# Batch 0 of an attention, mixture and Fourier kernel: q and k loaded as whole rows over two queues and turned by TensorE

## The chip, the cores and the metric

The kernel runs on one core of a Trainium2 chip. The metric is the time of one execution in device microseconds. A profile shows one execution; its span runs from the first to the last instruction, and that execution's own time is a little longer than its span.

## The reference

Three stages follow each other, in float32 (the weights of the second and third stage come as 8-byte numbers and are narrowed on the chip):

```python
# q, k, v: batch 4, 8 heads, 576 positions, head size 64
q_d, k_d, v_d = (mean over 4 neighbouring positions of q, k, v)          # 144 positions
out_up    = repeat(softmax(q_d k_d^T / 8) v_d, 4)
out_local = softmax(q k^T / 8, masked to |i - j| < 4) v
x = out_up + out_local                     # (4, 576, 512)
h = relu(x @ w_in);  u, v = halves of h;  v_n = layernorm(v)
x = (u * (w_spatial @ v_n + b_spatial)) @ w_out
u = x + real(fft2(x))
out = u + relu(layernorm(u) @ w_ch1) @ w_ch2
```

Both score products of the attention need q and k with the head size on the partitions, that is, turned: in memory a position's 64 numbers lie side by side.

## The kernel before

The attention works in halves: batch b, group g of four heads. A half has four tiles of 128 partitions by 576 columns (two of q, two of k, two heads in each: partitions 0 to 63 and 64 to 127). The steps of a half are short functions, named in an order string (`ORD0` for batch 0): T turns a tile, PD pools it over four positions (POOL), BS makes the masked local scores and their softmax, PS the pooled ones, BA and PA turn the probabilities, BV and PV multiply by v and add into `xf`, the attention's output of the batch.

`moe(b)` is the second and third stage up to the Fourier transform of batch b. It is nearly all TensorE work: each product is done as three matmuls on a high and a low part (`mm3`, lines 138 to 141). The attention of batch b+1 is woven into moe(b) by a planner (`Filler`) that deals out steps by costs given in the code. The feed-forward (`ffn_gen`) comes last. Before moe(0) can start, the attention of batch 0 has to be done (both of its halves run interleaved, lines 1065 to 1077) and w_in has to be brought into `winh` and `winl`.

Loads are issued by SP, in program order: all eight q/k tiles of batch 0 first (line 1051), then v in two layouts (`vb`, `vp`) mixed with the sixteen loads of w_in into eight staging pieces (`prep_fetch`, lines 1052 to 1062), then q, k and v of batch 1. A q/k tile comes in by four DMAs (`qk_load`, line 326), each of which takes 32 of a head's 64 columns: runs of 32 numbers, 128 bytes, laid so that a transposition of 32x32 blocks within DVE (line 406) ends with the head size on the partitions.

w_in is narrowed piece by piece (`narrow`, lines 118 to 130: one ACT operation at 124, three DVE operations at 125, 126 and 128), then ACT casts the high part into `winh` (line 198) and POOL subtracts for the low part in `winl` (line 185).

The order in which an engine gets its instructions is set when the program is built, by a scheduler that follows a simulated timeline; on the chip each engine then works in that order. PSUM tiles of the first half come from the tags `tp` (two banks), `sc` (two) and `av` (one), those of the second half from `mm` (three).

Of the kernel before, what the change touches and what calls it, by code (L numbers as in the profile page):

```python
# [9 lines left out]
F32 = mybir.dt.float32  # L10
F32R = mybir.dt.float32r
# [8 lines left out]
P = 128  # L20
# [2 lines left out]
EPS = 1e-6  # L23
RATIO = [0.35, 0.5, 0.55, 0.5]
QK, T2 = 7, 6
EARLY = 12
PREP0 = 18
BVE = 'aa'
# [16 lines left out]
def tile_attn_moe_fft_mixer(  # L45
# [18 lines left out]
    nc = tc.nc  # L64
    B, H, S, D = q.shape
# [9 lines left out]
    big = ctx.enter_context(tc.tile_pool(name="big", bufs=1))  # L75
# [10 lines left out]
    def bank(tag, shape):  # L86
        n = 1
        for s in shape[1:]:
            n *= s
        t = ps.tile([P, 512], F32, tag=tag, name=tag, bufs={"mm": 3, "tp": 2, "sc": 2, "av": 1}[tag])  # L90
        t = t[:shape[0], :n]
        if len(shape) == 3:
            t = t.rearrange("p (a b) -> p a b", a=shape[1])
        elif len(shape) == 4:
            t = t.rearrange("p (a b c) -> p a b c", a=shape[1], b=shape[2])
        return t
# [18 lines left out]
    def wide(src):  # L115
        return 1 if src.dtype == F32 else 2

    def narrow(raw, n, scratch=None):
        w = raw.rearrange("p (n two) -> p n two", two=2)
        m = t2(n) if scratch is None else scratch[0]  # L120
        mi = m.bitcast(I32)
        a = t2(n) if scratch is None else scratch[1]
        ai = a.bitcast(I32)
        nc.scalar.mul(m, w[:, :, 1], 2.0 ** -112)  # L124
        nc.vector.tensor_scalar(ai, mi, 3, 0x7FFFFFF8, op0=ALU.logical_shift_left, op1=ALU.bitwise_and)  # L125
        nc.vector.scalar_tensor_tensor(ai, in0=mi, scalar=-2 ** 31, in1=ai, op0=ALU.bitwise_and,  # L126
                                       op1=ALU.bitwise_or)
        nc.vector.scalar_tensor_tensor(ai, in0=w[:, :, 0].bitcast(I32), scalar=29, in1=ai,  # L128
                                       op0=ALU.logical_shift_right, op1=ALU.bitwise_or)
        return a  # L130
# [13 lines left out]
    ident = ident_r.bitcast(F32)  # L144
# [7 lines left out]
    folds = const.tile([97, 66], F32R, name="folds")  # L152
    fold, fold_o = folds[:, 0:33], folds[:, 33:66]

    winh = big.tile([P, 4, 1024], F32R, tag="winh", name="winh")
    winl = big.tile([P, 4, 1024], F32R, tag="winl", name="winl")
    wsh_, wf_, ds_, dd_ = [], [], [], []

    u2_d = [[dram.tile([S, DM], F32, name=f"u2_d{b}_{i}") for i in range(4)] for b in range(B)]
# [24 lines left out]
    def prep_lo(lo, w, hi):  # L184
        LOENG.tensor_tensor(lo, w, hi.bitcast(F32), op=ALU.subtract)

    def prep():
        dbl = wide(w_in)
        sg = big.tile([P, 4, 512], F32, tag="wfl", name="scratch")
        prev = None  # L190
        for n in range(8):
            h, kk = 1 - n // 4, n % 4
            c = slice(h * 512, (h + 1) * 512)
            w = stage[n][:, :512 * dbl]
            if dbl == 2:
                w = narrow(w, 512, (sg[:, 2 * (n % 2), :], sg[:, 2 * (n % 2) + 1, :]))
            hi = winh[:, kk, c]
            nc.scalar.copy(hi, w)
            if prev is not None:
                prep_lo(*prev)  # L200
            prev = (winl[:, kk, c], w, hi)
            yield
        prep_lo(*prev)
        yield
# [78 lines left out]
    ready = {}  # L283
# [7 lines left out]
    def aux(kind, alt, m=None):  # L291
        shape, bufs = SPEC[kind]
        if not alt:
            t = ap_.tile(shape, F32, tag=kind, name=kind, bufs=bufs)
        else:
            tag, off, n = ALT[kind]
            if tag not in alt_tiles:
                alt_tiles[tag] = big.tile([P, ALTSZ[tag]], F32, tag=tag, name="alt_" + tag)
            size = 1
            for x in shape[1:]:  # L300
                size *= x
            i = alt_n.get(kind, 0)
            alt_n[kind] = i + 1
            o = off + (i % n) * size
            t = alt_tiles[tag][:shape[0], o:o + size]
            if len(shape) == 3:
                t = t.rearrange("p (a b) -> p a b", a=shape[1])
            elif len(shape) == 4:
                t = t.rearrange("p (a b c) -> p a b c", a=shape[1], b=shape[2])
        return t if m is None else t[:, 0:m]  # L310
# [3 lines left out]
    def is_alt(b, g):  # L314
        return b == 0 and g == 1

    extra = {}

    def qk_load(b, g, t):
        x = aux("qk", is_alt(b, g))  # L320
        src, hp = (q, k)[t % 2], t // 2
        for h2 in range(2):
            for dh in range(2):
                pt = 64 * h2 + 32 * dh
                h = b * H + 4 * g + 2 * hp + h2
                nc.sync.dma_start(x[pt:pt + 32].rearrange("p (j c) -> p j c", c=32),  # L326
                                  bass.AP(src.tensor, h * S * D + 32 * dh, [[D, 32], [32 * D, S // 32], [1, 32]]))
        ready["n", b, g, t] = x
# [30 lines left out]
    UNITS = [(0, 1), (2, 3), (4,)]  # L359
    bg = [(b, g) for b in range(B) for g in range(2)]  # L360
    loader = {"n": qk_load, "vp": vp_load, "vb": vb_load}
    queues = {}
    for alt in (False, True):
# [10 lines left out]
    def abank(tag, alt, shape):  # L374
        return bank("mm" if alt else tag, shape)
# [20 lines left out]
    def half(b):  # L396
        st = {}
# [4 lines left out]
            return xf_t[b]  # L402

        def t_(g, t):
            x = ready.pop(("n", b, g, t))
            nc.vector.transpose(x, x)  # L406
            st["qk", g, t] = x
# [112 lines left out]
        def bv_out(g, u, av, m):  # L520
# [13 lines left out]
            else:  # L534
                acc(xs[:, :, 467:525], av[:, :, 0, 3:61])
                acc(xs[:, :, 525:576], av[:, :, 1, 13:64])

        return {"T": (t_, .1), "PD": (pd, 0.2), "PS": (ps_, 1.0), "PA": (pa, .5), "PV": (pv, .95), "BS": (bs, 3.0),
                "BA": (ba, .45), "BV": (bv, 2.7)}

# [520 lines left out]
    for _ in pf:  # L1061
        pass
    pr = itertools.chain(prep(), prep_sp())
    atg = attention()
    ga, gb = head_half(0, bg[2]), head_half(1, None)
    live = [ga, gb]
    n = early = 0
    while live:
        for x in list(live):
            if next(x, "end") == "end":  # L1070
# [2 lines left out]
        if n > PREP0:  # L1073
            next(pr, None)
        if ga not in live and early < EARLY:
            next(atg)
            early += 1
    for _ in pr:
        pass
    for _ in range(EARLY - early):  # L1080
        next(atg)
# [91 lines left out]
```

## Time and profile before

| | |
|---|---|
| median of 3 runs | 865.77 us (861.98 to 866.14) |
| the profiled execution: its time, its span | 863.39 us, 861.6 us |
| busy in the span | PE 804.5, DVE 485.9, ACT 304.5, POOL 192.4 us |
| mean granted TensorE clock | 0.972 of full speed |
| moved by DMA | 71.84 MB in 154209 packets, 122805 of them under 512 B |
| first matmul of moe(0) | 79.31 us |

Times are microseconds from the span's start. PE is TensorE's matmuls, PEld its weight loads, DVE is VectorE, ACT ScalarE, POOL GpSimd, SP the engine that issues most of the DMAs. A slice of the page is a fortieth of the span, 21.5 us; its digit is the busy share in tenths.

### The profile page before, as it was taken

To read this page: it belongs to the slowest core of one execution; us is meant where nothing else is said; L and a number is where in the kernel's file an instruction comes from. 1 tells how busy PE (TensorE), PEld (TensorE's weight loads), DVE (VectorE), ACT (ScalarE), POOL (GpSimd) and SP (SyncE) were. 2 spreads that over 40 slices of the span, in tenths; PEclk is the share of its full clock that TensorE was granted. 3 is DMA by queue.
4 is the path that set the end of the run, shared out by engine and by line. 5 is a ranking of instruction groups with operands and counts; after the bars stand their busy time and mean duration, and the time that the engine had idled before them with its cause. 6 is when DMAs were issued, how large, how long until landed. Compare 5 with 4: busy or idle time off the path is not lost.

```text
span 861.6 us, 14351 instructions
## 1 busy us (share of the span) xinstructions
PE 804.5 (93%) x5309; PEld 664.9 (77%) x5309; DVE 485.9 (56%) x1109; ACT 304.5 (35%) x929; POOL 192.4 (22%) x237
## 2 busy tenths in 40 slices
PE   3658999999999999999799889999999999999998
PEld 1547888778977897899587667888888888888897
DVE  3798899587578846669749995223222322221211
ACT  1764774445363627334524552111110111111011
POOL 4457522224123310133504552000000000000000
PEclk9677999999999999999899899999999999999999
DMA  7788364433233110152406552322121222110100
GB/s 121 186 175 191 73 141 114 83 88 62 53 70 92 38 33 1 35 174 70 152 22 201 187 172 75 109 49 58 40 98 40 59 49 83 40 25 0 49 1 25
DMA packets 154209, 71.84 MB, mean 83 GB/s; under 512 B 122805, under 2 KB 140822, under 8 KB 154140
## 3 DMA queue, kind: packets, MB, share of 16 engines
q1 hardware_dynamic: 152668, 65.63, 31.0%
q0 software_dynamic: 1472, 5.30, 1.9%
q8 instruction: 42, 0.69, 0.3%
q14 instruction: 27, 0.22, 0.1%
HBM read 58.83 MB, written 12.07 MB: 82 GB/s over the span
## 4 chain that ended last, share of the span: by engine, by line
PE 75%; DVE 12%; SPq 4%; issue 3%; DMA 3%; ACT 2%; POOL 1%; DVEq 0%; ACTq 0%; POOLq 0%
PE mm L139 15%; PE mm L140 14%; PE mm L141 14%; PE tp L141 4%; PE tp L139 4%; PE tp L140 4%; PE sc L139 3%; PE sc L140 3%; PE sc L141 3%; SPq L326 2%; DVE t L128 2%; PE sc L433 2%; DVE t L126 2%; DVE t L125 1%; PE sc L481 1%
## 5 line engine op out<-in xcount | busy, mean ns | idle before, releaser
L964 DVE SCALAR_TENSOR_TENSOR hl<-mm,hh 128x512 fp32r<-128x512 f32 (+1 forms) x80 | 50.9, 636 | 220.2 <-ACT hh L589 220.2
L589 ACT ACTIVATE hh<-mm 128x512 fp32r<-128x512 f32 (+1 forms) x80 | 44.3, 554 | 264.6 <-PE mm L141 260.0
L599 POOL TENSOR_TENSOR rs<-ve,nhalf 128x1 f32<-128x1 f32 (+1 forms) x38 | 25.3, 679 | 251.0 <-DVE ve L598 246.8
L386 ACT ACTIVATE eb<-sc,mx 128x64 f32<-128x64 f32 x140 | 41.7, 340 | 32.2 <-DVE mx L384 32.1
L139 PE MATMUL mm<-xgh,winh 128*128 128x288 f32 x128 | 39.2, 307 | 0.0
L139 PE MATMUL mm<-wfh,xgh 128*128 128x512 f32 (+1 forms) x80 | 33.8, 423 | 5.4 <-ACT yx L705 5.3
L139 PE MATMUL mm<-wsh,vnh 128*128 128x288 f32 x128 | 38.4, 300 | 0.0
L140 PE MATMUL mm<-xgl,winh 128*128 128x288 f32 x128 | 38.2, 298 | 0.0
L141 PE MATMUL mm<-xgh,winl 128*128 128x288 f32 x128 | 38.1, 297 | 0.0
L140 PE MATMUL mm<-wsl,vnh 128*128 128x288 f32 x128 | 38.0, 297 | 0.0
L141 PE MATMUL mm<-wsh,vnl 128*128 128x288 f32 x128 | 38.0, 297 | 0.0
L128 DVE SCALAR_TENSOR_TENSOR t<-raw,t 128x512 int32<-128x512 int32 x32 | 36.3, 1134 | 0.0
L406 DVE STREAM_TRANSPOSE qk<-qk 128x576 f32<-128x576 f32 x28 | 21.7, 775 | 23.3 <-DMA qk<-in_q_dram 12.8
L386 ACT ACTIVATION_READ_ACCUMULATOR eb<-sc,mx 128x1 f32 x140 | 32.6, 233 | 0.0
L140 PE MATMUL mm<-wfl,xgh 128*128 128x512 f32 (+1 forms) x80 | 32.5, 409 | 0.0
L423 POOL TENSOR_TENSOR ta<-qk 128x288 f32<-128x288 f32 x28 | 22.9, 818 | 40.1 <-DVE qk L406 34.0
L141 PE MATMUL mm<-wfh,xgl 128*128 128x512 f32 (+1 forms) x80 | 31.3, 410 | 0.0
L816 POOL DMA_INDIRECT u_d<-t,idx x12 | 15.6, 1298 | 61.9 <-DVE t L809 55.6
L124 ACT ACTIVATE t<-raw 128x512 f32<-128x512 f32 x32 | 21.3, 671 | 20.7 <-DMA raw<-in_moe_w_ch_dram 11.6
L411 POOL TENSOR_TENSOR vp<-vp 72x512 f32<-72x512 f32 x13 | 17.8, 1368 | 45.8 <-DMA vp<-in_v_dram 45.8
L481 PE MATMUL sc<-qk 64*64 64x64 f32 x560 | 20.4, 246 | 8.0 <-DMA qk<-in_q_dram 3.9
L383 DVE TENSOR_REDUCE mx<-sc 72x2 f32<-72x288 f32 (+2 forms) x49 | 24.3, 506 | 5.1 <-PE sc L433 4.4
(526 smaller groups left out, 2525.9 us busy)
## 6 DMA issues: line engine op xcount, KB each, us to landing
raw<-in_moe_w_ch_dram SPq DMA_DIRECT2D x32, 512.0 KB
out_dram<-t SPq DMA_DIRECT2D x18, 256.0 KB
qk<-in_q_dram SPq DMA_DIRECT2D x56, 72.0 KB
qk<-in_k_dram SPq DMA_DIRECT2D x56, 72.0 KB
vp<-in_v_dram SPq DMA_DIRECT2D x26, 144.0 KB
vb<-in_v_dram SPq DMA_DIRECT2D x56, 64.0 KB
u2t<-u_d SPq DMA_DIRECT2D x10, 256.0 KB
t<-u_d SPq DMA_DIRECT2D x10, 256.0 KB
```

The costliest lines, as they stand in the source:

```text
L128: nc.vector.scalar_tensor_tensor(ai, in0=w[:, :, 0].bitcast(I32), scalar=29, in1=ai, op0=ALU.logical_shift_right, op1=ALU.bitwise_or)
L139: nc.tensor.matmul(out, lhsT=ah, rhs=bh, start=first, stop=False)
L140: nc.tensor.matmul(out, lhsT=ah, rhs=bl, start=False, stop=False)
L141: nc.tensor.matmul(out, lhsT=al, rhs=bh, start=False, stop=last)
L383: nc.vector.reduce_max(mx, sc, axis=AX.X)
L386: nc.scalar.activation(e[:, i, :], sc[:, i, :], AF.Exp, bias=mx[:, i:i + 1], scale=sc_in, accum_out=sm[:, i:i + 1])
L406: nc.vector.transpose(x, x)
L423: E['pd'].tensor_tensor(a, x[:, 0::2], x[:, 1::2], op=ALU.add)
L481: nc.tensor.matmul(scs[u][c, z, :], lhsT=x[2 * hp][o, s:s + 64], rhs=x[2 * hp + 1][o, s:s + 64], start=False, stop=(i == 2 * m - 1 and hp ...
L589: nc.scalar.activation(dst, src, AF.Relu)
L599: nc.gpsimd.tensor_tensor(rs, ve, nhalf[:rows], op=ALU.pow)
L964: last[0] = nc.vector.scalar_tensor_tensor(hl[:, :n], in0=ph, scalar=0.0, in1=hh[:, :n].bitcast(F32), op0=ALU.max, op1=ALU.subtract)
```

## The change

The q and k tiles of batch 0 (both halves) are loaded otherwise and turned otherwise; those of batches 1 to 3 stay. A tile is now loaded by two DMAs, one head each, the first issued by SP and the second by ACT. A partition takes nine neighbouring positions of a head, all 64 columns of each: one run of 576 numbers, 2304 bytes. These raw rows lie in the memory of `winl` (seven tiles) and `winh` (the eighth); `winh` and `winl` themselves are therefore allocated later, in `prep`. Step T of batch 0 (`qk_turn`) takes 18 matmuls against the identity (nine positions by two heads, 64x64 each) into two PSUM tiles, and two copies, of five positions by ACT and of four by DVE, that write to every ninth column. The main loop now draws the four T steps of both halves ahead of everything else, and the counter that starts the preparation of w_in starts at 4 to match.

```diff
-    winh = big.tile([P, 4, 1024], F32R, tag="winh", name="winh")
-    winl = big.tile([P, 4, 1024], F32R, tag="winl", name="winl")
+    winh = winl = None
...
     def prep():
+        nonlocal winh, winl
+        winh = big.tile([P, 4, 1024], F32R, tag="winh", name="winh")
+        winl = big.tile([P, 4, 1024], F32R, tag="winl", name="winl")
...
+    homes = {}
+
+    def qk_rows(b, g, t):
+        src, hp = (q, k)[t % 2], t // 2
+        n = 4 * g + t
+        tag = "winl" if n < 7 else "winh"
+        if tag not in homes:
+            homes[tag] = big.tile([P, 4096], F32, tag=tag, name="rows_" + tag)
+        raw = homes[tag][:, S * (n % 7):S * (n % 7) + S]
+        for h2 in range(2):
+            h = b * H + 4 * g + 2 * hp + h2
+            (nc.sync, nc.scalar)[h2].dma_start(raw[64 * h2:64 * h2 + 64],
+                                               bass.AP(src.tensor, h * S * D, [[S, 64], [1, S]]))
+        ready["n", b, g, t] = raw
+
+    def qk_turn(b, g, t):
+        raw = ready.pop(("n", b, g, t))
+        x = aux("qk", is_alt(b, g))
+        xr = x.rearrange("p (s r) -> p r s", r=NR)
+        for r0, n, copy in ((0, 5, nc.scalar.copy), (5, 4, nc.vector.tensor_copy)):
+            tp = abank("tp", is_alt(b, g), [P, n, 64])
+            for r in range(n):
+                for h2 in range(2):
+                    o = slice(64 * h2, 64 * h2 + 64)
+                    nc.tensor.matmul(tp[o, r, :], lhsT=raw[o, (r0 + r) * D:(r0 + r + 1) * D], rhs=ident[o, o],
+                                     start=True, stop=True)
+            copy(xr[:, r0:r0 + n, :], tp)
+        return x
+
     def qk_load(b, g, t):
+        if b == 0:
+            qk_rows(b, g, t)
+            return
...
         def t_(g, t):
+            if b == 0:
+                st["qk", g, t] = qk_turn(b, g, t)
+                return
...
-    n = early = 0
+    for x in live:
+        for _ in range(4):
+            next(x)
+    n, early = 4, 0
```

## Rows read from the trace of the kernel before

**Rows 1.** The page's slices: PE, tenths busy in each fortieth of the span.

```profile
PE   3658999999999999999799889999999999999998
```

**Rows 2.** Table by stage: busy us (instructions) per engine, clock, DMA share, GB/s.

```profile
0.00:28.00 28.00, 11.80 (x152) 8.27 (x152) 10.64 (x24) 7.50 (x37) 10.58 (x26) 1.00 0.77 138
...
35.00:80.00 45.00, 31.63 (x354) 24.44 (x353) 43.68 (x86) 30.74 (x107) 28.59 (x26) 0.69 0.84 178
80.00:861.60 781.60, 758.92 (x4772) 630.18 (x4770) 425.90 (x989) 262.63 (x766) 150.09 (x184) 0.99 0.29 75
```

**Rows 3.** Timeline of PE: start, duration, instructions, idle time before and its releaser.

```profile
9.16 0.69 PE L481 MATMUL sc<-qk 64*64 64x64 f32 x8 [3.87 <-DMA qk<-in_q_dram]
13.24 1.98 PE L481 MATMUL sc<-qk 64*64 64x64 f32 x56 [3.39 <-DVE qk L406]
...
79.31 0.79 PE L139 MATMUL mm<-winh,xgh 128*128 128x512 f32 x1
```

**Rows 4.** The chain of waits at the head: start, duration, what it ran through.

```profile
1.65 0.42 SPq L326
...
18.90 0.74 SPq L354
...
27.32 3.95 DMA stage_vyh<-in_moe_w_in_dram
...
31.82 2.49 ACT alt_wsh L386 x16
```

**Rows 5.** Timeline of DVE: first and last of batch 0's eight transpositions.

```profile
6.34 0.78 DVE L406 STREAM_TRANSPOSE qk<-qk 128x576 f32<-128x576 f32 x1 [2.77 <-DMA qk<-in_q_dram]
...
20.88 0.78 DVE L406 STREAM_TRANSPOSE alt_xgh<-alt_xgh 128x576 f32<-128x576 f32 x1 [1.17 <-DMA alt_xgh<-in_k_dram]
```

**Rows 6.** Timeline of ACT: its first exponential, and the first piece of w_in.

```profile
19.73 0.31 ACT L386 ACTIVATE eb<-sc,mx 128x64 f32<-128x64 f32 x1 [16.48 <-DVE mx L384]
...
27.35 0.66 ACT L124 ACTIVATE scratch<-stage_vyh 128x512 f32<-128x512 f32 x1 [2.77 <-DMA stage_vyh<-in_moe_w_in_dram]
```

**Rows 7.** DMA issues of the whole span: tile, queue, count, size of one.

```profile
qk<-in_q_dram SPq DMA_DIRECT2D x56, 72.0 KB
...
vb<-in_v_dram SPq DMA_DIRECT2D x56, 64.0 KB
...
stage_vyh<-in_moe_w_in_dram SPq DMA_DIRECT2D x4, 256.0 KB
```

**Rows 8.** Timeline of SP: q of batch 1 issued right behind w_in.

```profile
50.71 5.45 SPq L326 DMA_DIRECT2D qk<-in_q_dram  x4
```

**Rows 9.** Table by stage: DMA's last two columns, busy share and GB/s.

```profile
15.00:20.00 5.00, 1.99 (x20) 1.33 (x14) 3.19 (x7) 0.27 (x2) 2.47 (x5) 1.00 0.86 139
...
50.00:55.00 5.00, 0.00 (x0) 0.00 (x0) 4.93 (x13) 1.45 (x7) 2.79 (x3) 0.79 1.01 233
```

**Rows 10.** Operations that read 128x256 from PSUM: ACT's by line, DVE's by time.

```profile
L496 ACT COPY eb<-tp 128x256 f32<-128x256 f32 x1 | 0.4, 382 | 0.0
```

```profile
53.51 0.40 DVE L383 TENSOR_REDUCE mx<-sc 128x4 f32<-128x256 f32 x1
...
108.06 0.54 DVE L107 TENSOR_TENSOR wsl<-tp,wsh 128x256 fp32r<-128x256 f32 x2
```

**Rows 11.** Narrowing of w_in on DVE, POOL beside it; sums of L126, then L128.

```profile
58.10 0.69 DVE L126 SCALAR_TENSOR_TENSOR scratch<-scratch 128x512 int32<-128x512 int32 x1
58.82 1.82 DVE L128 SCALAR_TENSOR_TENSOR scratch<-stage_uy,scratch 128x512 int32<-128x512 int32 x1
...
67.38 1.45 POOL L411 TENSOR_TENSOR vp<-vp 72x512 f32<-72x512 f32 x1
67.73 2.26 DVE L126 SCALAR_TENSOR_TENSOR scratch<-scratch 128x512 int32<-128x512 int32 x1
...
0.00:80.00 80.00, 7.40 (x8) 0.79 0.80 162
...
0.00:80.00 80.00, 9.31 (x8) 0.79 0.80 162
```

More of the change, by code (lines that the diff above doesn't have):

```diff
@@ L25 @@
 QK, T2 = 7, 6
+NR = 9
 EARLY = 12
```

## The prediction

> **What bounds the kernel now.** I read the page's slices first [rows 1]: PE is busy in nine tenths or more nearly everywhere, and its idle time lies in the first four slices of 21.5 us. The table by stage says the same in numbers [rows 2]: from 80 us to the end PE is busy 758.9 of 781.6 us (97%), before that 45.6 of 80. So a change at the head is worth what it moves the start of the long PE stretch. That start is the first matmul of moe(0), at 79.31 us [rows 3].
>
> What sets that start changes on the way. From 35 to 80 us DVE is busy 43.7 of 45 us: DVE is the bound there. From 0 to 28 us it is busy only 10.6 us [rows 2]. The chain of waits names what comes ahead of the DVE stretch [rows 4]: SP's queue without a gap from 1.65 to 27.3 us (its 32 issues for q and k first, at 0.54 us each, then v and w_in), then the landing of the second piece of w_in at 31.27, then DVE, ACT and PE in turns. The engines' own rows show the same: all eight q/k tiles are on DVE one by one, the first at 6.34, the last at 20.88 us [rows 5]; ACT sits idle from 24.6 to 27.35 us for the first piece of w_in while the softmax of the second half waits behind it, in order, until 31.82 [rows 4, 6]. The head is thus a feeding problem up to about 31 us and a DVE problem after it.
>
> **The change part by part.** *Loads.* 32 loads of 72 KB [rows 7] in runs of 128 bytes (2.36 MB) become 16 of 144 KB in runs of 2304 bytes, eight on SP and eight on ACT. SP gets back 24 issues of 0.54 us: its first load of v is issued at about 6.0 us instead of 18.90 [rows 4], 12.9 us earlier, and all behind it moves up while the transfers keep pace. They may not. While the 128-byte loads run alone the DMA engines are 0.86 busy for 139 GB/s; at 50 to 55 us, with mostly whole rows of w_in in flight, share 1.01 gives 233 GB/s [rows 9]. No row shows 2304-byte runs alone; between the two ends they are nearer to w_in's rows, so I take 233. Then the q/k bytes need 10.1 us (17.0 at 139). With 2.2 us to the end of the first issue and the 2.0 us that lie today between the last issue's end (18.86) and the last tile's transposition (20.88), the last tile is there at 14.3 us: 6.6 earlier. At 139 GB/s it would be 21.2 us (no gain), with issue alone as the limit 1.65 + 8 × 0.54 + 2.0 = 8.0 us (12.9 earlier).
>
> What speaks against counting the second queue for more than its issues: SP's queue by itself fills the DMA engines at 50 to 55 us [rows 9]. The Trainium skill, page "DMA: Bandwidth & Descriptors", section "Issuing engines are not separate DMA queues", says that loads started from several engines run on the same 16 DMA engines and save only the time to start them. By that rule the 14.3 us stand; if the second queue brought a rate of its own the last tile would be there at about 9.3 us and the kernel at some 853. The trace agrees with the rule as far as it goes, with no load on ACT in it.
>
> *What follows on SP.* The first piece of w_in has 3.15 MB in front of it and in it (q/k, four loads of v of 64 KB, two of w_in of 256 KB [rows 7]): 13.5 us at 233 GB/s, so about 17.7 us against 27.35 [rows 6], 9.6 earlier (2.7 if q/k stay at 139; 13 if only the issue counts). The second piece, 4.23 MB, comes at 22.4 against 31.27: 8.9 earlier. This is the term that the chain runs through.
>
> *The turn.* Eight DVE transpositions of 0.778 us go (6.2 us) [rows 5]. In their place each tile has 18 matmuls of 64x64, a copy of 128x320 out of PSUM by ACT and one of 128x256 by DVE. PE: the nearest rows are 35 ns each (56 in 1.98 us) and 86 ns each (8 in 0.69) [rows 3], so 0.6 to 1.5 us a tile and 5 to 12 us in all, which PE's 16 idle us of the first 28 cover [rows 2]. DVE: 0.40 us by its reduction of 128x256 out of PSUM, and 0.27 by a subtraction of that size (two in 0.54) [rows 10]; no row writes with a stride of nine elements, so the upper bound is the old 0.778. I take 0.40: 3.0 us less in all, in a stretch where DVE is idle anyway, so nothing, and 3 us where it isn't. ACT: its copy of 128x256 takes 0.38 us [rows 10], so some 0.41 for 320 columns (0.48 if it grew in proportion), 3.3 us in all, and its eight issues. No row has an issue on ACT: between nothing and SP's slow 1.36 us each (four in 5.45) [rows 8]; I take 0.54, so 4.3 us. Together 7.6 us beside an idle stretch of ACT from 3.25 to 19.73 [rows 6]. If the issues cost 1.36 us, ACT is free at about 14 us and the last half tile comes at about 16: still 5 earlier. A tile's way through PE and copy is 1.0 to 1.9 us instead of 0.78; I take 0.7 us more, so the q/k path gains 5.9.
>
> *The rest.* The old order of the eight tiles (first half, then second) was already the one on the chip, so the new loop ahead of the halves moves nothing that counts. The staging of the raw rows in the two tiles of winh and winl is free long before those are first written (the first narrowed piece of w_in, at 27.35 today, cannot precede the load). Of batch 1 to 3 nothing changes.
>
> **The sum.** Two feeds come earlier, q/k by 5.9 us and w_in by about 9. The DVE stretch needs both. ACT runs the first half's exponentials before w_in's first piece in either order, so its wait of 2.8 us shrinks and the second half's softmax follows directly. I take 8 us for the start of the DVE stretch, hence for the start of moe(0) (79.31 to about 71), and PE's stretch behind it, 97% full, moves as a whole. The profiled execution took 863.39 us (span 861.6 and 1.8 around it); 863.4 − 8 = 855.4. The median shown is 2.4 us above that execution, so the new median would be about 858.
>
> **Rivals.** *A, the first scores wait for all eight tiles.* In program order the turns of both halves now stand ahead of the first half's scores, and PE works in order. Then scores that begin in earnest at 13.24 us [rows 3] begin at 14.3 + 1.9 = 16.2, the softmax on ACT starts no earlier than today's 19.73, and only ACT's wait of 2.8 us goes: 865.8 − 2.8 = 863. For it: the order in the code; against it: today's engine order follows the tiles' arrival, not the code, which interleaves the halves.
>
> *B, slower: DVE pays beside POOL.* The narrowing of w_in is pulled forward into the stretch in which POOL adds up q, k and v. The same DVE operation takes 0.69 us at 58.10 and 2.26 at 67.73, where POOL starts an addition on v at 67.38; the operation after it takes 1.82 at 58.82 [rows 11]. The eight pairs sum to 7.40 + 9.31 = 16.7 us now [rows 11]. At 2.26 + 1.82 each they would be 32.6: 15.9 us more on the engine that bounds the head, minus 8, so 865.8 + 8 = 874. The sign turns where a pair exceeds 3.1 us in the mean (2.1 now). Against it: without the one of 2.26 the other seven of the first kind take 0.73 in the mean, though POOL is busy 28.6 of the 45 us [rows 2, 11]. The Trainium skill, page "SBUF — State Buffer", section "SBUF: two separate sides", describes this as an exclusive lock: a DVE instruction with two SBUF inputs and a POOL instruction block each other for a whole instruction. The rows at 58.82 and 67.73 are as it would have them.
>
> *C, issue is the limit.* If whole rows move faster than 233 GB/s, w_in comes 13 us earlier and DVE's 3 us count partly: 865.8 − 14 = 852.
>
> *D, the loads stay slow.* If a 2304-byte run costs per byte what the short ones do, q/k gain nothing and w_in 2.7: 863, as A.
>
> **How the numbers follow.** 0.5% is 4.3 us, about what a measurement of this kernel can tell from no change. Forecast (4.5 to 11 us gained): 0.60. C: 0.08. A and D together: 0.20. B: 0.12, of which a quarter ends within 0.5%. So faster 0.68, same 0.23, slower 0.09. The range reaches from 850 (C with all of DVE's 3 us) to 866 (no gain at all), which leaves out most of B and little below.
>
> **What would show it.** On SP: v's first load at 6 us. A DMA rate above 200 GB/s before 15 us. The first piece of w_in used by ACT at about 18 us, with little wait. DVE full from about 27 us; the first matmul of moe(0) at about 71 us, and PE's busy time behind it unchanged near 759 us. The forecast is wrong if moe(0) starts where it did (A, D), if the pair of DVE operations exceeds 3 us (B), or if moe(0) starts early and PE's later stretch grows idle.

## The result and the profile after

The kernel became slower: 871.19 us in the median of 4 runs (869.87 to 873.07), against 864.96 (861.98 to 866.14, 4 runs) for the kernel before on the same chip. The ratio is 1.0074, 95% interval 1.005 to 1.0098. The predicted 858 us had the wrong sign. The profiled execution took 873.07 us, its span 871.3.

The table by stage of the kernel after, which answers to [rows 2, 9] (window, length, then busy us and instructions of PE, PEld, DVE, ACT and POOL, granted clock, DMA share, GB/s):

```profile
0.00:28.00 28.00, 15.64 (x302) 14.13 (x304) 9.91 (x19) 8.64 (x13) 10.29 (x20) 0.85 0.82 181
28.00:35.00 7.00, 3.56 (x130) 2.70 (x123) 2.34 (x4) 2.32 (x4) 6.71 (x11) 0.74 0.82 200
35.00:80.00 45.00, 28.42 (x274) 21.57 (x274) 41.88 (x95) 30.50 (x140) 28.21 (x24) 0.56 0.87 168
80.00:871.30 791.30, 763.92 (x4906) 634.81 (x4903) 433.76 (x994) 268.08 (x781) 144.82 (x184) 0.99 0.28 73
5.00:10.00 5.00, 3.53 (x54) 2.90 (x54) 0.61 (x1) 0.73 (x1) 0.62 (x1) 1.00 1.04 243
```

The whole rows do load fast: 243 GB/s between 5 and 10 us, where 233 had been taken. Yet from 28 to 35 us DVE and ACT work for only 2.3 of 7 us each. That is the hole the change tore, in the stretch in which DVE had been expected to become full.

PE's timeline after, answering to [rows 3]: the first tile's turn, the last ones, the scores of the first half, and the start of moe(0).

```profile
6.24 2.19 PE L346 MATMUL tp<-ident_r,rows_winl 64*64 64x64 f32 x36 [0.77 <-DMA rows_winl<-in_q_dram]
...
20.74 1.12 PE L346 MATMUL tp<-ident_r,rows_winl 64*64 64x64 f32 x16 [4.59 <-DVE qk L348]
21.65 2.77 PE L346 MATMUL mm<-ident_r,rows_winl 64*64 64x64 f32 x46
25.84 2.08 PE L346 MATMUL mm<-ident_r,rows_winh 64*64 64x64 f32 x34 [1.42 <-DVE alt_xgh L348]
...
27.77 1.96 PE L519 MATMUL sc<-qk 64*64 64x64 f32 x62
...
88.89 0.50 PE L140 MATMUL mm<-winh,xgh 128*128 128x512 f32 x1
```

The bulk of the first half's scores begins 14.5 us later than before (27.77 against 13.24), moe(0) 9.6 us later (88.89 against 79.31). The stretch behind is as long as it was: 871.3 − 88.89 = 782.4 us, 861.6 − 79.31 = 782.3. So the head alone lost, as the head alone had been expected to gain. Of the 9.7 us between the two spans 6.2 are left in the medians; the profiled execution is the longest of the four.

ACT's timeline after, answering to [rows 6]:

```profile
19.05 0.66 ACT L125 ACTIVATE scratch<-stage_vyh 128x512 f32<-128x512 f32 x1 [3.98 <-DMA stage_vyh<-in_moe_w_in_dram]
19.61 0.72 ACT L348 COPY qk<-tp 128x320 f32<-128x320 f32 x1
...
24.09 0.67 ACT L125 ACTIVATE scratch<-stage_vyh 128x512 f32<-128x512 f32 x1 [3.19 <-DMA stage_vyh<-in_moe_w_in_dram]
24.65 0.72 ACT L348 COPY alt_xgh<-mm 128x320 f32<-128x320 f32 x1
...
30.73 0.61 ACT L219 CAST vn4a<-rb 2x512 fp32r<-2x512 f32 x1 [2.76 <-POOL rb L218]
31.36 1.14 ACT L201 CAST winh<-scratch 128x512 fp32r<-128x512 f32 x2
...
37.96 0.62 ACT L201 CAST winh<-scratch 128x512 fp32r<-128x512 f32 x1 [4.89 <-DVE scratch L129]
...
40.04 0.31 ACT L421 ACTIVATE eb<-sc,mx 128x64 f32<-128x64 f32 x1 [0.90 <-DVE mx L419]
```

DVE's and POOL's timelines after: DVE's waits, the first maximum of the softmax, and the two subtractions on POOL for which DVE waits.

```profile
19.74 0.43 DVE L126 TENSOR_SCALAR scratch<-scratch 128x512 int32<-128x512 int32 x1 [5.38 <-ACT scratch L125]
20.08 0.61 DVE L348 COPY qk<-tp 128x256 f32<-128x256 f32 x1
...
33.71 1.47 DVE L126 TENSOR_SCALAR scratch<-scratch 128x512 int32<-128x512 int32 x1 [4.66 <-POOL winl L185]
...
37.85 1.27 DVE L418 TENSOR_REDUCE mx<-sc 128x8 f32<-128x512 f32 x2
```

```profile
32.40 2.50 POOL L185 TENSOR_TENSOR winl<-scratch,winh 128x512 fp32r<-128x512 f32 x2
```

These rows hold the cause. ACT's narrowing of w_in's first piece (19.05) now stands ahead of its copies of the last tiles (19.61 and on), and ACT works in order: it waits 3.98 us for the load while those copies wait behind. DVE does the same (19.74, then the copy at 20.08), and so PE's turns stop for 4.59 us. After the turns the softmax still doesn't follow. ACT first has the cast of `vn4a` and those of w_in; DVE first has the third piece's narrowing, which waits 4.66 us for the scratch that POOL's subtractions free. The first maximum comes at 37.85 us (17.48 before), the first exponential at 40.04 (19.73 [rows 6]). Of these 20.3 us 9.6 are left at the start of moe(0).

SP's timeline after, answering to [rows 4]: its last loads of rows, the first of v, the first of w_in.

```profile
6.71 0.58 SPq L333 DMA_DIRECT2D rows_winl<-in_k_dram  x1
9.34 0.47 SPq L333 DMA_DIRECT2D rows_winl<-in_q_dram  x1
9.85 0.60 SPq L333 DMA_DIRECT2D rows_winh<-in_k_dram  x1
10.49 2.63 SPq L389 DMA_DIRECT2D vb<-in_v_dram  x4
13.17 1.26 SPq L114 DMA_DIRECT2D stage_vyh<-in_moe_w_in_dram  x1
```

The groups of the turn after (busy us, mean ns of one; then the idle time before them):

```profile
L346 PE MATMUL tp<-ident_r,rows_winl 64*64 64x64 f32 x144 | 7.5, 269 | 6.1 <-DVE qk L348 5.3 <-DMA rows_winl<-in_q_dram 0.8
L346 PE MATMUL mm<-ident_r,rows_winl 64*64 64x64 f32 x108 | 6.4, 291 | 0.4 <-DMA rows_winl<-in_q_dram 0.4
L348 ACT COPY qk<-tp 128x320 f32<-128x320 f32 x4 | 2.9, 730 | 7.6 <-PE tp L346 7.6
L348 DVE COPY qk<-tp 128x256 f32<-128x256 f32 x4 | 2.4, 612 | 4.1 <-PE tp L346 4.1
L346 PE MATMUL mm<-ident_r,rows_winh 64*64 64x64 f32 x36 | 2.2, 314 | 1.4 <-DVE alt_xgh L348 1.4
```

The 144 matmuls leave 144 + 108 + 36 = 288 records, two each. The groups sum to 16.1 us; where records of two groups that overlap in time are counted once, PE is busy 14.7 us with them.

Narrowing of w_in on DVE, the sums of L127 and L129, answering to [rows 11]:

```profile
0.00:80.00 80.00, 7.12 (x8) 0.68 0.84 176
...
0.00:80.00 80.00, 8.72 (x8) 0.68 0.84 176
```

The eight pairs take 15.8 us, 0.9 less than before: DVE doesn't pay beside POOL.

### The profile page after: what moved, and what is told of

Its sections match the earlier page's. It is cut to its first block, busy times and chain, and to the rows that moved or that the text cites. A ratio compares the mean times of both kernels' runs of the same rounds, so it can differ in the third digit from the quotient of the medians.

```text
span 871.3 us, 14880 instructions
## 1 busy us (share of the span) xinstructions
PE 811.5 (93%) x5597; PEld 673.2 (77%) x5597; DVE 487.9 (56%) x1109; ACT 309.5 (36%) x937; POOL 190.0 (22%) x237
## 4 chain that ended last, share of the span: by engine, by line
PE 72%; DVE 13%; SPq 5%; DMA 4%; issue 3%; ACT 2%; POOL 1%; DVEq 0%; another core or an unknown queue 0%; ACTq 0%
PE mm L140 14%; PE mm L142 14%; PE mm L141 14%; PE tp L142 4%; PE tp L141 4%; PE tp L140 4%; PE sc L140 3%; PE sc L141 3%; PE sc L142 3%; DVE t L129 2%; SPq L389 2%; PE sc L471 2%; DVE t L127 2%; SPq L361 2%; DVE t L126 1%
## 5 line engine op out<-in xcount | busy, mean ns | idle before, releaser
L637 POOL TENSOR_TENSOR rs<-ve,nhalf 128x1 f32<-128x1 f32 (+1 forms) x38 | 23.2, 627 | 250.1 <-DVE ve L636 246.1
L129 DVE SCALAR_TENSOR_TENSOR t<-raw,t 128x512 int32<-128x512 int32 x32 | 35.3, 1103 | 0.0
L471 PE MATMUL sc<-qd 64*72 64x144 f32 x112 | 20.4, 312 | 13.8 <-ACT eb L421 11.1
L471 PEld LDWEIGHTS sc<-qd 64*72 64x72 f32 x112 | 13.7, 149 | 19.7 <-issue 16.2
L444 DVE STREAM_TRANSPOSE qk<-qk 128x576 f32<-128x576 f32 x24 | 18.6, 773 | 18.2 <-DMA qk<-in_q_dram 10.1
```

Source lines behind the costliest of these rows:

```text
L471: nc.tensor.matmul(sc[:, j, :], lhsT=qd[o, 2 * hp, j * JH:(j + 1) * JH], rhs=qd[o, 2 * hp + 1, :], start=True, stop=True)
L637: nc.gpsimd.tensor_tensor(rs, ve, nhalf[:rows], op=ALU.pow)
```

## Experiments

The theory, T in the expectations and T2 once its list of waits had grown: the loss is order. Work that waits for transfers, or for other engines, stands ahead of batch 0's softmax in the queues of ACT, DVE, POOL and PE. Its rivals: the turn on PE or its copies are too slow, the loads or the second queue are, or DVE has simply more to do. Ratios are to the kernel before on the same chip, with 95% intervals. "Behind X" in a diff is the builder's mark that an instruction is put after X in its engine's queue.

### Which part of the change does it

**x13_no_loop**: the edit of the main loop taken out of the changed kernel.

```diff
-    for x in live:
-        for _ in range(4):
-            next(x)
-    n, early = 4, 0
+    n = early = 0
```

> The changed kernel without its last edit: the loop that draws the four T steps of both halves ahead of everything else is taken out, loads and turns stay. T2 (the order follows the planned times of the new loads and turns, not the place of T in the program): ACT, DVE and PE still get batch 0's softmax behind the narrowing of w_in's first pieces, the first exponential runs at 37 to 41 us, moe(0) starts at 87 to 90, 870 to 873 us, ratio 1.005 to 1.010. Rival A (the loop puts all turns ahead of the first scores and so costs the time): the first scores on PE follow the first half's four tiles, before 22 us, the first exponential by 30, moe(0) before 84, about 865 us, ratio under 1.003.

Measured: 872.09 us, 1.0077 [1.0048, 1.0107]. Its ACT:

```profile
18.50 0.66 ACT L125 ACTIVATE scratch<-stage_vyh 128x512 f32<-128x512 f32 x1 [3.17 <-DMA stage_vyh<-in_moe_w_in_dram]
...
39.22 0.31 ACT L421 ACTIVATE eb<-sc,mx 128x64 f32<-128x64 f32 x1 [0.62 <-DVE mx L419]
```

As T2 said, the same late softmax without the loop edit; the bulk of the first scores still comes behind the turns of both halves, at 29.17 us. So the new loads and turns are enough for the new order on the engines. The likely reason is that w_in comes earlier in the scheduler's simulated time and so is narrowed first; no run shows it, and none parts the loads from the turns.

**x4_one_queue**: all sixteen loads of rows on SP. **x5_two_queues**: the kernel before, with its old column-block loads shared by SP and ACT.

```diff
-            (nc.sync, nc.scalar)[h2].dma_start(raw[64 * h2:64 * h2 + 64],     # x4
+            nc.sync.dma_start(raw[64 * h2:64 * h2 + 64],
...
-                nc.sync.dma_start(x[pt:pt + 32]...                            # x5, on the kernel before
+                (nc.sync, nc.scalar if b == 0 else nc.sync)[h2].dma_start(x[pt:pt + 32]...
```

> The changed kernel with all sixteen loads of whole rows on SP, none on ACT: the second queue alone is undone. Theory T and T2 (the order on the engines decides, not the feed): last of the loads 1 to 4 us later at most (eight more issues of 0.54 us on SP), first load of v issued at 10 to 12 us as now, moe(0) within 3 us of 88.89, 869 to 875 us (ratio 1.004 to 1.011). Rival R3 (two queues share the completions and hold each other up): faster than the changed kernel by 2 us or more, 869 us or less. Also possible by chance of the planner: with other load times in its plan the order of the narrowing changes, which the positions of w_in's first piece among the tile copies would show.

> The kernel before with one part of the change alone: the column-block loads of batch 0's q and k are split over SP and ACT (16 issues each); the turn stays on DVE and the order on ACT and DVE stays that of the kernel before. If the number of issues on SP held up w_in: first load of v issued at about 10 to 11 us instead of 18.90, the first piece of w_in used by ACT at about 22 to 23 us instead of 27.35, moe(0) 2 to 5 us earlier than 79.31, 860 to 863 us (ratio 0.995 to 0.998). If the 128-byte runs fill the DMA engines (139 GB/s at 0.86 busy) and what comes earlier on SP only shares with them: q/k tiles later by 1 to 3 us, w_in at 24 or later, 864 to 867 us (ratio 0.999 to 1.003).

Measured: x4 872.56 us, 1.0075 [1.0046, 1.0103], the same as the change with two queues (1.0074). x5 865.31, 0.9989 [0.9972, 1.0006], no different from before. In x4 ACT uses w_in's first piece at 20.28 us instead of 19.05, and moe(0) starts at 88.22. SP issues its sixteen loads there one every 0.64 us and v's first at 11.88 us: taking half of them off SP gained 1.4 us, not the time of eight issues. In x5 moe(0) starts at 77.01, 2.3 us earlier than before, but the stretch behind it is longer (788.0 us against 782.3), and DVE waits there:

```profile
82.08 0.78 DVE L406 STREAM_TRANSPOSE qk<-qk 128x576 f32<-128x576 f32 x1 [5.14 <-DMA qk<-in_q_dram]
```

That is batch 1's q. The second queue is neither the harm nor a gain. The Trainium skill, page "DMA: Bandwidth & Descriptors", section "Issuing engines are not separate DMA queues", has it that loads from several engines share the same DMA engines and save only the time to start them; x4 and x5 agree (1.0075 against 1.0074 and 0.9989).

### Taking the waits away one after the other

**x1_order**: narrowing put behind the last tile's two copies.

```diff
-                w = narrow(w, 512, ...)
+                with tc.issue_after(turned[0].ins), tc.issue_after(turned[5].ins):
+                    w = narrow(w, 512, ...)
```

> The changed kernel, with one thing added: the narrowing of w_in on ACT and DVE may not be issued until the last of the sixteen copies of turned tiles has been, on either engine. Nothing else is named, but the softmax still follows behind two narrowed pieces. Theory T (the loss is the order on ACT and DVE: pieces of w_in stand between the copies and hold them up): copies without the gaps of 3.98, 5.38, 3.19 and 4.66 us, PE's turns ended by about 20 us instead of 27.9, the first maximum on DVE at about 30 us instead of 37.85, moe(0) at 80 to 84 us instead of 88.89, and a time of 862 to 867 us (ratio to the kernel before 0.996 to 1.002). Rival R1 (the turn itself, by its PSUM banks and its strided copies, is what is slow): the turns end after 25 us whatever stands between them, moe(0) at 87 us or later, 869 to 873 us (ratio 1.005 to 1.009). Rival R3 (the loads come late because two queues hold each other up): as R1, with PE waiting for rows and not for copies.

Measured: 884.40 us, 1.0221 [1.02, 1.0242], slower still. The turns end at 19.8 us without a stop, so neither PE nor the loads held them in the change. But the time didn't follow:

```profile
30.78 0.61 ACT L220 CAST vn4a<-rb 2x512 fp32r<-2x512 f32 x1 [6.43 <-POOL rb L219]
...
37.73 2.10 DVE L126 TENSOR_SCALAR scratch<-scratch 128x512 int32<-128x512 int32 x1 [7.53 <-POOL winl L185]
```

Two waits that the change has too grew: ACT's for the cast from 2.76 to 6.43 us, DVE's for POOL from 4.66 to 7.53. The first exponential runs at 37.99 us, moe(0) starts at 91.28. T's mechanism held for the turns, its time did not.

**v2_softmax_first**: narrowing behind half 0's exponentials on ACT and half 1's maxima on DVE, and four of batch 1's transpositions behind the last normalisation. **v3_half_first**: the same, and half 0's turns, sums and scores ahead of half 1's turns.

```diff
+                with tc.issue_after(marks[0]["exp"].ins), tc.issue_after(marks[1]["mx"].ins):   # v2
+                    w = narrow(...)
...
-        for _ in range(4):                                                                     # v3
+        for _ in range(6):
```

> The changed kernel with the narrowing of w_in issued only behind the exponentials of the first half's first scores (ACT) and the maxima of the second half's (DVE), and the transposes of batch 1's first half only behind the last normalisation, so that they do not move up into the gap. Theory T: the first maximum on DVE at about 21 us (37.85 in the changed kernel, 17.48 before), the first exponential at about 22 (40.04 and 19.73), moe(0) at 74 to 80 us, and 856 to 863 us (ratio 0.990 to 0.998): faster than both. Rival R1 (the turn itself is slow): first exponential after 27 us, moe(0) at 83 us or later, 866 us or more (ratio 1.002 or more). Rival R4 (DVE as a whole bounds the head, whose sum of work is the same in any order): moe(0) near 79 as in the kernel before, 863 to 866 us.

> As v2_softmax_first, and the first half's turns, scores and products drawn ahead of the second half's: the second half's turn matmuls may be issued on PE only behind the first half's first scores. Theory T with the recorded prediction's rival A (scores of the first half wait for all eight tiles): the first scores at about 14 us instead of 21, the first exponential at about 16, moe(0) 2 to 6 us ahead of v2_softmax_first's if the softmax of the first half is what the head waits for; 853 to 860 us (ratio 0.986 to 0.994). If DVE's work or w_in's second piece bounds the head by then, no gain over v2_softmax_first (within 1.5 us).

Measured: v2 878.05 us, 1.0147 [1.0123, 1.0171]; v3 880.34, 1.0173 [1.0153, 1.0193]. Of v2:

```profile
30.41 0.61 ACT L220 CAST vn4a<-rb 2x512 fp32r<-2x512 f32 x1 [10.24 <-POOL rb L219]
31.04 0.32 ACT L423 ACTIVATE eb<-sc,mx 128x64 f32<-128x64 f32 x1
...
59.49 1.47 DVE L126 TENSOR_SCALAR scratch<-scratch 128x512 int32<-128x512 int32 x1 [12.58 <-POOL winl L185]
```

The maxima are there at 22.46 us, yet ACT holds the exponentials back for one cast of 2x512 numbers, whose memset stands on POOL behind sums that wait for v. Later DVE waits 12.58 us for POOL, which stands 12.98 us before batch 1's v. In v3 the first exponential runs at 17.85 us, but half 1's turns then stand behind half 0's pooled scores on PE, and DVE waits 7.82 us at 58.95; moe(0) starts at 94.79.

**v5_all_waits_behind**: v3 with those waits put behind too (the cast behind the exponentials, POOL's sums of v behind those of q and k, batch 1's behind `winl`, half 0's pooled scores behind half 1's scores), and half 1's tiles copied by DVE alone. **v7_tiles_then_softmax**: the same, but all eight tiles first and copied by ACT and DVE, as in the change.

```diff
+        with tc.issue_after(made["exp"].ins):
+            nc.scalar.copy(vn4a[64:66], oz[64:66])
...
+            with tc.issue_after(made["pd" if not b else "lo"].ins) if not b or made["lo"] else nullcontext():
+                E['vd'].tensor_tensor(x[:, :, :, 0:128], ...)
```

> The changed kernel with every kind of work that waits for a late transfer put behind the softmax of both halves, not w_in's narrowing alone: as v3_half_first, and in addition the cast that waits for POOL's clearing of a buffer of v is behind the exponentials traced so far, POOL's sums of v of batch 0 are behind its sums of q and k, those of batch 1 behind the last subtraction of w_in traced so far, the products of the first half's pooled q and k on PE are behind the second half's scores, and the second half's tiles are copied by DVE alone, so that ACT has the first half's exponentials at once. Theory T2 (the loss is waiting in order, on all four engines: whatever waits for a transfer and stands ahead of the softmax costs what it waits, and x1, v2 and v3 only uncovered the next one: 10.24 us on ACT for the cast in v2, 12.58 and 7.82 us on DVE for POOL's w_in subtraction behind batch 1's v in v2 and v3): first exponential at about 18 us, the second half's at 26 to 29, DVE without a wait of more than 4 us from 30 us on, moe(0) at 72 to 80 us, 855 to 865 us (ratio 0.988 to 1.000). Rival R5 (the head is bound by the sum of work on DVE and PE, which the turn makes larger: order changes nothing but its place): moe(0) at 86 us or later, 868 us or more (ratio 1.003 or more).

> As v5_all_waits_behind but with the changed kernel's own order of the eight tiles (all turned ahead of the first half's scores) and its own copies (ACT 320 columns, DVE 256). Theory T2: PE's turns ended at about 19.8 us as in x1_order, first exponential at about 23.5 us (31.04 in v2_softmax_first, where ACT waited for the cast), the second half's directly behind at about 28, moe(0) at 74 to 82 us, 857 to 867 us (ratio 0.990 to 1.002). If turning half by half is worth what the recorded prediction's rival A gave it, 2 to 4 us slower than v5_all_waits_behind. Rival R5: 868 us or more.

Measured: v5 876.04 us, 1.0114 [1.0084, 1.0145]; v7 874.97, 1.0109 [1.0081, 1.0137]. Of v7:

```profile
70.28 0.78 DVE L449 STREAM_TRANSPOSE qk<-qk 128x576 f32<-128x576 f32 x1 [8.18 <-DMA qk<-in_q_dram]
...
71.14 0.32 ACT L425 ACTIVATE alt_wsh<-mm,mx 128x64 f32<-128x64 f32 x1 [11.15 <-DVE mx L423]
```

One long wait is left: the transposition of batch 1's q stands on DVE ahead of batch 0's last work (10.47 us at 74.19 in v5).

**v8_transposes_behind**: v7 with batch 1's other four transpositions behind batch 0's last additions. **v9_halves_behind**: the same on v5.

```diff
-            with tc.issue_after(made["mul"].ins) if (b, g) == (1, 0) else nullcontext():
+            with tc.issue_after(made["xf" if g else "mul"].ins) if b == 1 else nullcontext():
                 nc.vector.transpose(x, x)
```

> As v7_tiles_then_softmax, and the transpositions of batch 1's second half, whose loads land at about 70 us, are put behind the additions that finish batch 0's attention on DVE traced so far (in v7 DVE waited 8.18 us for the first of them at 62 us, and ACT 11.15 us behind DVE, with two pieces of w_in still to narrow). Theory T2 (every wait in order ahead of moe(0) costs what it lasts, and this is the last large one): no wait over 3 us on DVE between 22 and 80 us, moe(0) at 78 to 83 us instead of 89.21, and 862 to 869 us (ratio 0.996 to 1.004): level with the kernel before, because the turned tiles come only some 2 us earlier than DVE's transpositions gave them. If the wait only moves once more: moe(0) at 86 us or later, 870 us or more. Rival R5 (the sum of work bounds the head): as the latter, with DVE busy over 42 of the 45 us from 35 to 80 us.

> As v5_all_waits_behind with the same transpositions put behind (in v5 DVE waited 10.47 us for the first of them). Theory T2: no wait over 4 us on DVE between 22 and 80 us, moe(0) at 78 to 84 us instead of 93.81, and 862 to 869 us (ratio 0.996 to 1.004); against v8_transposes_behind the first half's exponentials start 5 us earlier and the second half's 4 us later, so the two should lie within 3 us of each other. If the wait only moves once more: 870 us or more.

Measured: v8 865.44 us (12 runs), 0.9995 [0.9981, 1.0009]; v9 870.24, 1.0047 [1.0028, 1.0066]. v8's PE, ACT and DVE:

```profile
20.40 1.09 PE L530 MATMUL sc<-qk 64*64 64x64 f32 x57
...
24.01 0.31 ACT L429 ACTIVATE eb<-sc,mx 128x64 f32<-128x64 f32 x1 [3.11 <-DVE mx L427]
...
44.46 1.47 DVE L128 TENSOR_SCALAR scratch<-scratch 128x512 int32<-128x512 int32 x1 [4.29 <-POOL winl L189]
...
68.90 0.78 DVE L453 STREAM_TRANSPOSE qk<-qk 128x576 f32<-128x576 f32 x1 [0.90 <-DMA qk<-in_k_dram]
...
80.47 0.50 PE L144 MATMUL mm<-winh,xgh 128*128 128x512 f32 x1
```

With the same loads, turns and copies as the change, and order alone set by hand, the whole loss is gone; DVE is busy 34.9 of the 45 us from 35 to 80, against 43.7 before, so more work on DVE is no cause. One control is missing, the same marks on the kernel before: they also put batch 1's work behind batch 0's, so v8 shows that order can give the whole loss back, not that it undoes only what the change did. And there is no gain. The scores wait for all eight tiles and begin at 20.40 us instead of 13.24, the first exponential runs at 24.01 instead of 19.73, and moe(0) starts at 80.47. Half by half, in v9, the first exponential runs at 17.64 us, but the second half's at 30.30, as in v8 (30.00), and the whole is 4.8 us slower. Its turns wait on copies (2.35 us at 21.96), DVE waits for POOL (5.13 us at 46.82, where v8 has 4.29), and moe(0) starts at 82.64; which of these costs the time is not shown.

**v10_two_on_dve**: v8 with the first two subtractions for `winl` on DVE instead of POOL. **v11_last_tile_behind**: v10 with the transposition of the last tile of batch 1's first half traced last and put behind batch 0's last additions too.

```diff
+        made["nlo"] = made.get("nlo", 0) + 1                                                   # v10
+        eng = nc.vector if made["nlo"] <= 2 else LOENG
...
-ORD0 = '... BV2 T3 PV0 PV1'                                                                    # v11
+ORD0 = '... BV2 PV0 PV1 T3'
...
-            with tc.issue_after(made["xf" if g else "mul"].ins) if b == 1 else nullcontext():
+            with tc.issue_after(made["xf" if g or t == 3 else "mul"].ins) if b == 1 else nullcontext():
```

> As v8_transposes_behind, and the first two of w_in's eight last subtractions run on DVE instead of POOL. In v8 DVE waited 4.29 us (to 44.46 us) for the first of them, which stood behind a sum of v on POOL whose load landed at 40 us. Theory T2: that wait goes for 1.4 us of work on DVE (two subtractions of 0.68), so moe(0) at 77 to 79 us instead of 80.47 and 861 to 865 us (ratio 0.995 to 0.999). If the chain behind it (batch 1's loads at 69 us, PE at 72 us) is what moe(0) waits for, no change: moe(0) at 80 to 81.5 us, 865 to 867 us.

> As v10_two_on_dve, and the transposition of the last q/k tile of batch 1's first half, whose load landed at 68.9 us in v8, is traced and issued behind the additions that finish batch 0's attention too. If v10 only moves the wait to that load: 2 us or more faster than v10, moe(0) at 75 to 78 us, 858 to 863 us (ratio 0.992 to 0.997), the first version ahead of the kernel before. If not: within 1.5 us of v10.

Measured: v10 865.93 us, 0.9987 [0.9967, 1.0008]; v11 864.55 (12 runs), 0.9978 [0.9959, 0.9997]. In v10 the wait moved, as its second answer has it: DVE waits 6.14 us at 69.37 for batch 1's k, and moe(0) starts at 80.81. v11 is ahead of the kernel before by so little that it is no change by the bound of 0.5%. Its moe(0) starts at 74.83 us, 4.5 earlier than before, but its stretch behind takes 864.8 − 74.83 = 790.0 us instead of 782.3:

```profile
74.83 0.50 PE L144 MATMUL mm<-winh,xgh 128*128 128x512 f32 x1
...
82.27 0.78 DVE L457 STREAM_TRANSPOSE qk<-qk 128x576 f32<-128x576 f32 x1 [3.43 <-DMA stage_ddl<-in_moe_w_out_dram]
...
83.74 0.50 PE L146 MATMUL mm<-winh,xgl 128*128 128x512 f32 x1 [3.07 <-DVE xgl L108]
```

Again a transposition that waits holds up, on DVE, what PE needs, now `xgl`, for 3.07 us. In the first 20 us of the stretch PE is busy 16.9 us at a granted clock of 0.91, before 19.7 at 0.98. Part of the 7.7 us is the choice of executions: the profiled one is 2.1 us slower than v11's median, the one before 2.4 us faster than its own. The rest was not traced to its end.

### What a turn costs on PE

**v12_head0_transpose**: v11 with head 0's turns as TensorE's transpositions, one record each, in turn with head 1's matmuls. **v14_transposes_grouped**: the same, head by head. **v15_heads_grouped**: v11, all matmuls, head by head.

```diff
                 for r in range(n):
                     for h2 in range(2):          # v14, v15: these two loops the other way round
...
+                        if h2:                                                                 # v12, v14
+                            nc.tensor.matmul(tp[o, r, :], lhsT=w, rhs=ident[o, o], start=True, stop=True)
+                        else:
+                            nc.tensor.transpose(tp[o, r, :], w, ident[o, o])
```

> As the last version (last tile behind), with the nine turns of the first head of each tile as TensorE transpositions (one record each) in place of matmuls with the identity (two records each). If TensorE's records set when a tile is turned: 27 records a tile instead of 36, turns end at 16 to 18 us instead of 19.8, the first exponential about 2 us earlier, 861 to 864 us, ratio 0.993 to 0.997. If the loads or the two copies set it: turns end at 19 to 20 as before, 864 to 866 us, ratio 0.997 to 1.000.

> As the version with head 0's turns as transpositions, but head by head: per PSUM tile first the transpositions of head 0, then the matmuls of head 1, not in turn. If the 0.64 us per pair came of changing between the two kinds at every position: turns end at 15 to 18 us, moe(0) before 82 us, 861 to 865 us. If a 64x64 transposition is itself slow (0.24 us): 72 of them take 17 us and the turns end at 23 to 26 us, 866 to 870 us.

> As the version with the last tile behind, all turns as matmuls, but head by head in each PSUM tile. The same instructions on every engine in almost the same order. If the two heads' matmuls (partitions 0 to 63 and 64 to 127) overlap on TensorE when they alternate: turns end at 22 to 28 us instead of 18.7, ratio 1.002 to 1.010. If they don't overlap: turns end at 18 to 20 us and 0.996 to 1.000 as before.

Measured: v12 898.33 us, 1.038 [1.0339, 1.042]; v14 883.58, 1.0209 [1.018, 1.0238]; v15 864.95, 0.9979 [0.9965, 0.9994]. PE in v12, in v14 and in v15 (L362 is the transposition, L360 and L358 the matmul):

```profile
12.95 0.31 PE L362 MATMUL tp<-ident_r,rows_winl 64*64 64x64 f32 x1 [0.70 <-DVE qk L363]
13.19 0.47 PE L360 MATMUL tp<-ident_r,rows_winl 64*64 64x64 f32 x2
13.59 0.31 PE L362 MATMUL tp<-ident_r,rows_winl 64*64 64x64 f32 x1
```

```profile
6.28 0.71 PE L362 MATMUL tp<-ident_r,rows_winl 64*64 64x64 f32 x5 [1.34 <-DMA rows_winl<-in_q_dram]
6.92 1.32 PE L360 MATMUL tp<-ident_r,rows_winl 64*64 64x64 f32 x10
```

```profile
6.39 2.97 PE L358 MATMUL tp<-ident_r,rows_winl 64*64 64x64 f32 x36 [1.38 <-DMA rows_winl<-in_q_dram]
```

Every pair in v12 takes 0.64 us (12.95 to 13.59), and its turns end at 53 us. The granted clock is 1.00 in v11, v12, v14 and v15 while the tiles are turned, so the clock is not the difference. Neither of the two answers expected holds alone: grouped (v14), a transposition takes 0.13 us and a matmul of two records 0.25, together 0.38, so the other 0.26 of the 0.64 comes with changing kind at each position; but ten records of matmuls beside them take 1.3 us, where v15, also head by head, has 36 in 2.97 (some 0.8 for ten), and the turns still end at 35 us, later than either expectation. Fewer records were not a shorter turn. v15 shows what the order within a tile is worth: head by head the first tile takes 2.97 us, with the heads in turn 2.19 (6.24 in the change, the same in v11), and the turns end at 23.0 instead of 18.8 us. So the two heads' matmuls overlap when they alternate. The Trainium skill, page "TensorE: Matmul & The Clock Gate", section "Part 3: Packing small matmuls — row/col tiling", says that small matmuls on different rows of the array run at the same time; these two durations agree. So the first answer expected holds for the turns, and the second for the time: those 4 us cost v15 nothing (0.9979 as v11). That fits what v8 showed: the tiles' arrival alone does not set the end.

## Why the prediction was wrong

The step that failed is in the sum: "ACT runs the first half's exponentials before w_in's first piece in either order". It was read from the trace before and carried over to the new loads without a reason. On the chip ACT narrows w_in's first piece at 19.05 us and runs the first exponential at 40.04. With that step the rest of the sum turned round: w_in's narrowing, whose earlier start was counted as 8 us of gain, ran ahead of the softmax and held it up. x13 shows that the loads and turns did it by themselves, v8 that order alone gives the whole of the loss back (1.0074 to 0.9995). The sentence before, "the new loop ahead of the halves moves nothing that counts", was right for the loop (x13: 1.0077) and wrong in what it was used for.

Step by step:

- *Loads*: right in rate (243 GB/s for 233), too early in issue. SP's first v load came at 10.49 us, not 6.0; SP's rows show 2.6 us between the loads at 6.71 and 9.34, which no term had. With all sixteen on SP (x4) there is no such stop; what stops the issue with two queues is not shown.
- *What follows on SP*: near. w_in's first two pieces were used at 19.05 and 24.09 us, forecast 17.7 and 22.4, against 27.35 before.
- *The turn*: mis-sized. 18 matmuls are 36 records: the first tile took 2.19 us against at most 1.5 forecast. The rows that it was sized by (8 and 56 of the first half's scores [rows 3]) are records too, 64 for 32 matmuls, and were read as one each. The sum is 14.7 us against 5 to 12, part of it at a granted clock of 0.50 (1.2 GHz) after PE had stood for 4.6 us; in x1, without that stop, it is 12.7. The copies took 0.61 us on DVE and 0.73 on ACT, forecast 0.40 and 0.41; the rows of reductions and of contiguous copies were the wrong neighbours. Where nothing stops them (x1) the turns end at 19.8 us and the last copy at 20.5. Before, the last transposition ended at 21.66. So the q/k path gains 1.2 us there, not 5.9.
- *PE's stretch behind moves as a whole*: right for a later start, 782.4 against 782.3 us. For an earlier one, which the forecast needed, the profiles speak against it: 788.0 us in x5 (start at 77.01), 786.0 in v15 (77.53), 790.0 in v11 (74.83). How much of a gain at the head the stretch takes back is open, as single executions of one kernel differ by some us (863.1 to 869.2 in the 17 runs of the kernel before beside x5).
- *Rival A*: its mechanism is real. In v8, with the other waits gone, the scores wait for all tiles until 20.40 us (forecast 16.2) and no gain is left; in the change they come at 27.77, because DVE's and ACT's copies stand behind the narrowing as well. Its price is not shown: v9, without that wait, is slower than v8.
- *Rival B* is refuted by the pair sum of 15.8 us, *C* by SP's 10.49 us and by moe(0), *D* by 243 GB/s. None of the four had the narrowing of w_in overtaking the softmax; the 0.09 given to slower stood on B alone.

Open: why v11, with moe(0) 4.5 us earlier, ends only 0.2% earlier. One wait of 3.07 us and a lower clock in the first 20 us are shown; the rest is not.

## What to carry to other kernels

Where a builder's planned timeline orders the engines' queues, an earlier transfer is also a new order: read from the program after, not from the code, what each in-order engine will do first, and price an early load by what it lets overtake the critical work. Removing one wait in such a queue uncovers the next; each of the five versions ahead of v8 did, until all that waits for late transfers stood behind batch 0's work. By then the load that came 8 us earlier was worth nothing: in v8 ACT narrows w_in's first piece at 28.66 us, behind the exponentials, where it did so at 27.35 before. And an earlier start of the long stretch is not yet an earlier end: look at what the stretch itself waits for.

## What was not expected of the hardware

A 64x64 float32 matmul against the identity leaves two records (288 for 144). Two heads' matmuls on partitions 0 to 63 and 64 to 127 overlap when they alternate (36 records in 2.19 us, 2.97 head by head). Transpositions in turn with matmuls take 0.64 us a pair, and the matmuls beside them are slower even when grouped (10 records in 1.3 us, against 36 in 2.97 without transpositions); why, no run here tells. A copy out of PSUM that writes every ninth column takes 0.61 us for 128x256 on DVE and 0.73 for 128x320 on ACT.
